# k loaded in long runs and put in order by a VectorE copy, squares made in place, weight words on the attention's load queue, in one core's fused attention and bilinear FFN

## The chip, the cores and the metric

The kernel runs on one core of one Trainium2 chip. The metric is the device time in microseconds (us), the median of the timed runs; the profile is of one more execution of the same program. The core's engines run side by side, each through its own list of instructions in order, and wait for each other by semaphores: TensorE (PE in the profile, with PEld for its weight loads), VectorE (DVE), ScalarE (ACT), GpSimd (POOL) and SyncE (SP), which here only issues DMA transfers. ACT issues DMA transfers too. The transfers of SP appear in the profile as queue q1, those of ACT as q10; both are carried by the same 16 DMA engines.

## The reference: attention with normalized q and k, then a bilinear FFN

```python
batch, n_heads, seq, head_dim = (8, 12, 448, 64)          # attention, fp32
def rmsnorm(x, g):
    rms = np.sqrt(np.mean(x * x, axis=-1, keepdims=True) + 1e-06)
    return x / rms * g
q_n, k_n = (rmsnorm(q, g_q), rmsnorm(k, g_k))
scores = scale * np.matmul(q_n, k_n.transpose(0, 1, 3, 2))
# ... softmax over the keys ...
return np.matmul(attn, v).astype(np.float32)

# bridge: (B,H,S,D) -> (B*S, H*D): 3584 tokens of 768
a = x @ w_a          # 768 x 1536
b = x @ w_b          # 768 x 1536
return (a * b @ w_out).astype(np.float32)                 # 1536 x 768
```

q, k and v are fp32; the FFN's weights arrive as float64 and are read by the kernel as pairs of 32-bit words.

## The kernel before

The kernel is written as a plan: every operation is noted with its engine, an estimated duration, a priority (`key`, smaller is earlier) and the tiles that it reads and writes; a list scheduler then fixes the order of each engine's list before anything runs. A tile has a tag, and a tag has a number of buffers: a new tile can be written only when the last user of the oldest one is done.

```python
# op(engine, us, key, emit, reads, writes, new=tiles opened, kb=..., dmas=...)
TURN = 0.18
LANES = 8
RATE, LANDING = 300.0, 2.0          # the planner's picture of a DMA
```

Attention goes in 24 steps `p` of four heads each. The 448 tokens of a head stand as 64 partitions of 7 tokens (token = 7 * partition + j). The loads of a step:

```python
def loads(p, nm):
    t = tile_of(f"{nm}{p}", nm, 2 if nm == "v" else 1)
    def emit():
        x = ld.tile([P, NT, 2, D] if nm == "k" else [P, 2, NT * D], FP32, tag=nm, ...)
        for w in range(2):
            pair = src[b, h0 + 2 * w:h0 + 2 * w + 2]
            nc.sync.dma_start(x[low_high[w]], pair.rearrange("h (p j) d -> p j h d" if nm == "k" else
                                                             "h (p j) d -> p h (j d)", j=NT))
    op("SP", 0.8 if nm != "k" else 1.4, p - (1.8 if nm == "v" else 2.0), emit, [], [t], new=[t],
       kb=460 if nm != "k" else 800, dmas=2)
```

q and v are read in runs of 7 * 64 * 4 = 1792 B, one for a partition and head. k is put in the order (j, head, d) by the transfer itself, because TensorE transposes two heads of one j together; its runs are 64 * 4 = 256 B. Then normalization:

```python
def normalize(p):                    # key = p - NORM, NORM = 2.5
    def squares(s, nm):
        sq = tile_of(f"sq{nm}{p}", "sq", 1)                  # one buffer for q's and k's squares
        # ACT: sq = Square(x); DVE: rs[p][:, s] = sum over d of sq
        op("ACT", 1.07, key, square, [f"{nm}{p}"], [sq], new=[sq])
        op("DVE", 1.1, key, lambda: nc.vector.tensor_reduce(rs[p][:, s], xs["sq", nm, p], AX, ALU.add), [sq], ...)
    # roots: DVE: mean + 1e-6; POOL: power -0.5     (once for q, once for k)
    # apply: DVE: qn = q * root of q, in the order (j, head, d)   (k's root goes into the exponential's scale)

def transposes(p):
    # PE: pt = transpose of k (7 pieces), then of qn (7 pieces); ACT: copy pt to qkT, q's with the gains as scale
    x = xs["k", p] if n == 1 else qns[p]
    for j in range(NT):
        nc.tensor.transpose(t[:, j * P:(j + 1) * P], x[:, j].rearrange("p h d -> p (h d)"), ident)
```

The scores of a step, their exponentials and the products with v follow in 7 pieces j (`sc`, `ET`, `o`). The sums over the keys (`su`) are products with ones in the first 5 steps; later steps add the pieces up on DVE and POOL first (`ADD_UP`). `invert` spreads the sums over partitions by a small transfer (few<-rec), inverts them on DVE, writes them to DRAM (inv<-few) and brings them back to all partitions (rec<-inv); `divide` multiplies.

The weights are made beside attention. `factors(n)` loads the words of a part in two transfers of 768 KB on ACT's queue, rounds them (ACT once, DVE six times over 128 x 1536), forms sums and differences, and stores the result for the later passes (ACT's queue, 1344 KB):

```python
LOADS = "ACT"
KEEPS = "ACT"
def factors(n, key, early, after):
    for part in range(2):
        def load(part=part):
            queue[LOADS].dma_start(...)                      # words of w_a, w_b or w_out
        op(LOADS, 0.45, key - 0.75, load, after, [f"{row}/{part}"], kb=768)
    # rounding, sums and differences on ACT and DVE, then
    queue[KEEPS].dma_start(kept[n], sts[n]...)

GATES = [0, 2, 4, 4, 5, 5, 7, 7, 8, 8, 10, 10, 16, 18, 21, 21, 27, 32]   # number of the score piece it waits for
seq = [15, 13, 16, 12, 14, 0, 1, 2, 3, 4, 5, 6, 7, 8, 9, 10, 11, 17]     # 0-11: w_a, w_b; 12-17: w_out
def weights(at, after):
    for x, n in enumerate(seq):
        if at == GATES[x]:
            factors(n, x * 0.45 + 1.0, x < 2, [after])
```

The FFN works in four passes of two batches, in a scheme of seven instead of eight products per block; its products (`pq`, then `po`, `a` to `g`) have a lower priority than attention and run on TensorE whenever attention has nothing ready.

Of the kernel before, what the change touches and what calls it, by code (L numbers as in the profile page):

```python
# [9 lines left out]
FP32 = mybir.dt.float32  # L10
U32 = mybir.dt.uint32
I32 = mybir.dt.int32
AF = mybir.ActivationFunctionType
# [12 lines left out]
class Plan:  # L26
# [11 lines left out]
    RATE, LANDING = 300.0, 2.0  # L38
# [132 lines left out]
def kernel(  # L171
# [35 lines left out]
    nc = tc.nc  # L207
# [91 lines left out]
    def fast_body(ld, wk, ps_s, ps_o, ps_mm, dram):  # L299
        plan = Plan()  # L300
        op, tile_of = plan.op, plan.tile
        NORM = 2.5
# [9 lines left out]
        LOADS = "ACT"  # L312
# [3 lines left out]
        ADD_UP = [None, 'DVE', 'POOL', 'DVE', 'POOL', 'DVE', 'DVE']  # L316
# [104 lines left out]
        xs, rs, qns, qkTs, pts, scs, ETs, sums, sus, os_, quads, hTs = ({} for _ in range(12))  # L421
        low_high = [slice(0, D), slice(D, P)]

        def loads(p, nm):
            b, h0 = p // HC, 4 * (p % HC)
            src = {"q": q, "k": k, "v": v}[nm]
            t = tile_of(f"{nm}{p}", nm, 2 if nm == "v" else 1)

            def emit():
                x = ld.tile([P, NT, 2, D] if nm == "k" else [P, 2, NT * D], FP32, tag=nm, name=nm + "_sb", bufs=2 if nm == "v" else 1)  # L430
                for w in range(2):
                    pair = src[b, h0 + 2 * w:h0 + 2 * w + 2]
                    nc.sync.dma_start(x[low_high[w]], pair.rearrange("h (p j) d -> p j h d" if nm == "k" else
                                                                     "h (p j) d -> p h (j d)", j=NT))
                xs[nm, p] = x
            op("SP", 0.8 if nm != "k" else 1.4, p - (1.8 if nm == "v" else 2.0), emit, [], [t], new=[t],
               kb=460 if nm != "k" else 800, dmas=2)

        def normalize(p):
# [8 lines left out]
            def squares(s, nm):  # L448
                sq = tile_of(f"sq{nm}{p}", "sq", 1)

                def square():
                    x = xs[nm, p]
                    t = xs["sq", nm, p] = wk.tile([P, 2 * NT, D], FP32, tag="sq", name="sq")
                    flat = (x.rearrange("p h (j d) -> p (h j) d", d=D) if nm == "q" else
                            x.rearrange("p j h d -> p (j h) d"))
                    nc.scalar.activation(t, flat, AF.Square)  # L456
                op("ACT", 1.07, key, square, [f"{nm}{p}"], [sq], new=[sq])
# [8 lines left out]
            def apply():  # L466
                qns[p] = wk.tile([P, NT, 2, D], FP32, tag="qn", name="qn")
# [4 lines left out]
                    ALU.mult)  # L472
            squares(0, "q")
# [7 lines left out]
            qn = tile_of(f"qn{p}", "qn", 1)  # L481
            op("DVE", 1.15, key, apply, [f"{ms}/q", f"q{p}"], [qn], new=[qn], lock=True)
# [804 lines left out]
```

## Time and profile before

| | before |
|---|---|
| device time, median of 3 runs | 1550.15 us (1547.28 to 1551.54) |
| span of the profiled execution | 1548.6 us |
| attention steps 0 to about 10, with the first weights | 0 to 240 us |
| first FFN pass, almost alone on TensorE | 240 to 400 us |
| attention with FFN products between | 400 to 520 and 740 to 890 us |
| DMA packets | 128866, of which 57860 under 512 B |
| q, k, v: transfers of 224 KB | 48 each |
| words of the weights: transfers of 768 KB | 36 |

How to read it: a span is the time from the first to the last instruction of the profiled execution. An engine's busy time is the union of its instructions. TensorE's matrix products are pipelined and their ends are modelled. DMA share is the mean busy share of the 16 DMA engines in a stretch; it can read a little over 1. The chain of waits follows the last instruction back to whatever released it at each step.

### The profile page before, as it was taken

The page shows a single profiled execution, that of the slowest core. Times are in us where ns is not written, and L with a number is a line of the kernel's source. Part 1 is how long each engine was busy: PE and PEld are TensorE (multiplying, and loading weights), DVE is VectorE, ACT ScalarE, POOL GpSimd, SP SyncE. Part 2 cuts the span into 40 slices and gives each one's busy share as a digit, 9 for nine tenths or more (in the row PEclk, how much of TensorE's full clock was granted, in tenths as well). Part 3 has the DMA queues.
Part 4 walks back from the last instruction along what each step waited for, and adds up shares of the span by engine and source line. Part 5 has one row for each costly group of instructions (what it writes and reads, how often), then busy time and mean ns, then how long its engine had stood idle before and what let it go on. Part 6 is the DMA issues. An engine that isn't in the chain of part 4 may idle for free.

```text
span 1548.6 us, 18051 instructions
## 1 busy us (share of the span) xinstructions
PE 1506.9 (97%) x6996; PEld 822.6 (53%) x6996; DVE 813.7 (53%) x1179; ACT 400.7 (26%) x654; POOL 314.1 (20%) x166
## 2 busy tenths in 40 slices
PE   8988999999999999999999999999999999999998
PEld 5553345555444555555444455555547855555796
DVE  5877869888786412222587543222237622222583
ACT  6767661111567100000445500000041000000000
POOL 3426432111345200011244300000111001000000
PEclk9999999999999999999999999999999999999999
DMA  9897445644445542212345456121226742222343
GB/s 269 240 268 199 97 108 178 218 163 175 143 118 128 150 146 76 103 71 107 102 110 152 114 159 199 72 107 71 95 83 206 247 159 100 79 82 91 111 140 110
DMA packets 128866, 214.74 MB, mean 139 GB/s; under 512 B 57860, under 2 KB 108292, under 8 KB 119044
## 3 DMA queue, kind: packets, MB, share of 16 engines
q1 hardware_dynamic: 100708, 160.02, 35.0%
q10 hardware_dynamic: 28064, 53.48, 9.9%
q8 instruction: 57, 0.93, 0.2%
q14 instruction: 37, 0.30, 0.1%
HBM read 169.08 MB, written 44.21 MB: 138 GB/s over the span
## 4 chain that ended last, share of the span: by engine, by line
PE 82%; DMA 7%; DVE 5%; ACT 3%; issue 1%; POOL 1%; SPq 1%; ACTq 0%; DVEq 0%; POOLq 0%
PE pq L1003 48%; PE po L726 16%; PE sc L515 5%; PE o L537 4%; DMA q_sb<-in_q_dram 2%; PE g L901 2%; PE a L901 2%; ACT ET L521 2%; PE pt L494 2%; DMA rec<-inv 1%; PE b L901 1%; PE su L573 1%; PE e L901 1%; PE d L901 1%; DMA lraw<-in_moe_w_b_dram 1%
## 5 line engine op out<-in xcount | busy, mean ns | idle before, releaser
L1003 PE MATMUL pq<-x,st 128*128 128x448 f32 x2016 | 763.5, 540 | 0.9 <-ACT rec L586 0.9
L1003 PEld LDWEIGHTS pq<-x,st 128*128 128x128 f32 x2016 | 381.2, 190 | 379.5 <-issue 371.2
L521 ACT ACTIVATE ET<-sc,ms 128x448 f32<-128x448 f32 x336 | 191.7, 633 | 92.2 <-PE sc L515 65.6
L515 PE MATMUL sc<-qkT 64*64 64x448 f32 x1344 | 177.2, 544 | 18.0 <-ACT ET L521 10.6
L537 PE MATMUL o<-ET,v_sb 64*64 64x448 f32 x1344 | 187.2, 545 | 7.5 <-ACT ET L521 6.9
L464 POOL TENSOR_TENSOR ms<-ms,expo 128x14 f32<-128x14 f32 x48 | 145.6, 3037 | 188.3 <-DVE ms L462 187.6
L1051 POOL TENSOR_TENSOR hT<-hT,t 128x448 f32<-128x448 f32 x24 | 28.4, 1185 | 744.7 <-DVE t L1049 742.5
L726 PE MATMUL po<-st,hT 128*128 128x384 f32 x504 | 166.4, 487 | 0.0
L726 PEld LDWEIGHTS po<-st,hT 128*128 128x128 f32 x504 | 95.0, 190 | 67.9 <-issue 3.9
L551 POOL TENSOR_TENSOR sum<-sum,ET 128x896 f32<-128x896 f32 x38 | 81.4, 2141 | 139.1 <-ACT ET L521 97.0
L1025 ACT COPY hT<-pq 128x448 f32<-128x448 f32 x24 | 12.8, 532 | 372.9 <-PE pq L1003 372.9
L515 PEld LDWEIGHTS sc<-qkT 64*64 64x64 f32 x1344 | 58.1, 132 | 95.2 <-issue 34.8
L537 PEld LDWEIGHTS o<-ET,v_sb 64*64 64x64 f32 x1344 | 60.2, 132 | 87.9 <-ACT ET L521 42.2
L726 PE MATMUL po<-st,fin 128*128 128x384 f32 x264 | 89.9, 490 | 0.0
L551 DVE TENSOR_TENSOR sum<-sum,ET 128x896 f32<-128x896 f32 x57 | 62.8, 1101 | 26.6 <-POOL sum L551 19.4
L726 PEld LDWEIGHTS po<-st,fin 128*128 128x128 f32 x264 | 49.1, 190 | 39.0 <-issue 7.0
L1063 POOL TENSOR_TENSOR hT<-hT,t 128x448 f32<-128x448 f32 x48 | 58.5, 1219 | 53.7 <-DVE t L1060 45.5
L458 DVE TENSOR_REDUCE ms<-sq 128x14 f32<-128x896 f32 x48 | 51.8, 1079 | 27.7 <-ACT sq L456 27.5
L1056 DVE TENSOR_TENSOR hT<-U,pq 128x448 f32<-128x448 f32 x48 | 29.8, 621 | 66.5 <-PE pq L1003 66.5
L746 DVE TENSOR_TENSOR o_sb<-fin,po 128x384 f32<-128x384 f32 x36 | 20.0, 554 | 80.2 <-PE po L726 72.4
L1060 DVE TENSOR_TENSOR t<-U,pq 128x448 f32<-128x448 f32 x48 | 29.7, 619 | 59.6 <-PE pq L1003 57.3
L1028 ACT COPY t<-pq 128x448 f32<-128x448 f32 x24 | 12.8, 533 | 176.0 <-PE pq L1003 176.0
(117 smaller groups left out, 1297.0 us busy)
## 6 DMA issues: line engine op xcount, KB each, us to landing
st<-kept SPq DMA_DIRECT2D x36, 1344.0 KB
st<-kept_o SPq DMA_DIRECT2D x28, 1152.0 KB
kept<-st ACTq DMA_DIRECT2D x12, 1344.0 KB
ti<-kept_t SPq DMA_DIRECT2D x48, 288.0 KB
q_sb<-in_q_dram SPq DMA_DIRECT2D x48, 224.0 KB
k_sb<-in_k_dram SPq DMA_DIRECT2D x48, 224.0 KB
v_sb<-in_v_dram SPq DMA_DIRECT2D x48, 224.0 KB
rec<-inv SPq DMA_DIRECT2D x48, 224.0 KB
```

Source lines behind the costliest of these rows:

```text
L458: op("DVE", 1.1, key, lambda: nc.vector.tensor_reduce(rs[p][:, s], xs["sq", nm, p], AX, ALU.add), [sq], [f"{ms}/{nm}"])
L464: lambda: nc.gpsimd.tensor_tensor(msf(), msf(), expo[:, 0:2 * NT * (b - a)], ALU.pow), [], names)
L494: nc.tensor.transpose(t[:, j * P:(j + 1) * P], x[:, j].rearrange("p h d -> p (h d)"), ident)
L515: nc.tensor.matmul(t[low_high[w], e, 0:S], lhsT=qkTs[p][low_high[e], 1, j * P + w * D:j * P + (w + 1) * D], rhs=qkTs[p][low_high[e], 0, w ...
L521: nc.scalar.activation(E[:, e], scs[p, j][:, e, 0:S], AF.Exp, scale=rs[p][:, 1, 2 * j + e:2 * j + e + 1])
L537: nc.tensor.matmul(os_[p][low_high[e], w, 0:S], lhsT=xs["v", p][low_high[w], e, j * D:(j + 1) * D], rhs=ETs[p, j][low_high[w], e], start=( ...
L551: two[e].tensor_tensor(sums[p], sums[p] if j > 1 else ETs[p, 0], ETs[p, j], ALU.add)
L726: nc.tensor.matmul(held["po"][:, 0:HALF], lhsT=a[0]()[:, c], rhs=sts[beta, 12 + place_of[f]][:, c], start=(c == 0), stop=(c == MH - 1))
L901: nc.tensor.matmul(held[bank], lhsT=x()[:, c], rhs=y(c), start=(start and c == 0), stop=(stop and c == MI - 1), skip_group_check=True)
L1003: nc.tensor.matmul(banks[bank][:, 0:S], lhsT=sts[at][:, f, c * P:(c + 1) * P], rhs=quads[x][:, c], start=(start and c == 0), stop=(stop an ...
L1056: take("DVE", 0.68, lambda bank=bank, i=i, n=n: V.tensor_tensor(C(i, n), held["U"], PS(bank), ALU.add), [f"p{ident_}.{bank}", U], [hp[i]])
L1063: lambda i=i, n=n, nm=nm: two[TIMES].tensor_tensor(C(i, n), C(i, n), held[nm], ALU.mult), [t], [hp[i]],
```

## The change

k is loaded like q and v, in runs of 1792 B, into a buffer that was the squares'; a copy on VectorE puts it in the order (j, head, d) into the buffer that was k's. k's squares are then made in place, over the raw k, and q's squares in the buffer of qn, which the normalized q overwrites afterwards. So no memory is added. The aim is to spare the DMA engines k's short packets while the weights are streaming in. The words of the weights are now issued by SP, in one list with the attention's loads, instead of by ACT. The order in which the weight parts are made, the score pieces that they wait for, and several priorities are new: loads of q and k 1.5 steps ahead, of v 0.5, normalization 1.5 (2.5 before), the inversion of the sums one step earlier in priority.

```diff
-    RATE, LANDING = 300.0, 2.0
+    RATE, LANDING = 300.0, 2.5
-        NORM = 2.5
+        NORM = 1.5
-        LOADS = "ACT"
+        LOADS = "SP"
+        TURNS = "DVE"
-        ADD_UP = [None, 'DVE', 'POOL', 'DVE', 'POOL', 'DVE', 'DVE']
+        ADD_UP = [None, 'DVE', 'DVE', 'POOL', 'DVE', 'DVE', 'POOL']
 ...
         def loads(p, nm):
-            t = tile_of(f"{nm}{p}", nm, 2 if nm == "v" else 1)
+            home = {"q": "q", "k": "sq", "v": "v"}[nm]
+            t = tile_of(f"{nm}{p}", home, 2 if nm == "v" else 1)
 ...
-                    nc.sync.dma_start(x[low_high[w]], pair.rearrange("h (p j) d -> p j h d" if nm == "k" else
-                                                                     "h (p j) d -> p h (j d)", j=NT))
+                    nc.sync.dma_start(x[low_high[w]], pair.rearrange("h (p j) d -> p h (j d)", j=NT))
-            op("SP", 0.8 if nm != "k" else 1.4, p - (1.8 if nm == "v" else 2.0), emit, [], [t], new=[t],
-               kb=460 if nm != "k" else 800, dmas=2)
+            op("SP", 0.8, p - (0.5 if nm == "v" else 1.5), emit, [], [t], new=[t],
+               kb=460, dmas=2)
+
+        def turn_over(p):
+            kn = tile_of(f"kn{p}", "k", 1)
+            def emit():
+                kns[p] = ld.tile([P, NT, 2, D], FP32, tag="k", name="kn", bufs=1)
+                to, x = kns[p].rearrange("p j h d -> p h j d"), xs["k", p].rearrange("p h (j d) -> p h j d", d=D)
 ...
+                    two[TURNS].tensor_copy(to, x)
+            op(TURNS, {"ACT": 1.07, "DVE": 1.0, "POOL": 1.9}[TURNS], p - NORM, emit, [f"k{p}"], [kn], new=[kn], lock=TURNS != "ACT")
 ...
             def squares(s, nm):
-                sq = tile_of(f"sq{nm}{p}", "sq", 1)
 ...
+                    if nm == "q":
+                        qns[p] = wk.tile([P, NT, 2, D], FP32, tag="qn", name="qn")
+                        t = qns[p].rearrange("p j h d -> p (j h) d")
+                    else:
+                        t = x
+                    nc.scalar.activation(t, x, AF.Square)
 ...
-                    x = xs["k", p] if n == 1 else qns[p]
                     for j in range(NT):
-                        nc.tensor.transpose(t[:, j * P:(j + 1) * P], x[:, j].rearrange("p h d -> p (h d)"), ident)
+                        x = (kns if n else qns)[p][:, j]
+                        nc.tensor.transpose(t[:, j * P:(j + 1) * P], x.rearrange("p h d -> p (h d)"), ident)
 ...
-            op("SP", 0.8, p - 0.0, spread_out, [t], [few], new=[few], kb=20, dmas=2)
+            op("SP", 0.8, p - 1.0, spread_out, [t], [few], new=[few], kb=20, dmas=2)
 ...      (the inversion's other operations likewise: p - 0.0 becomes p - 1.0)
-        GATES = [0, 2, 4, 4, 5, 5, 7, 7, 8, 8, 10, 10, 16, 18, 21, 21, 27, 32]
-        seq = [15, 13, 16, 12, 14, 0, 1, 2, 3, 4, 5, 6, 7, 8, 9, 10, 11, 17]
+        GATES = [1, 2, 3, 4, 4, 6, 6, 7, 10, 10, 10, 13, 14, 16, 17, 17, 20, 24]
+        seq = [12, 16, 14, 13, 15, 0, 1, 2, 3, 4, 5, 6, 7, 8, 9, 10, 11, 17]
 ...
-                    factors(n, x * 0.45 + 1.0, x < 2, [after])
+                    factors(n, x * 0.65 + 0.0, x < 2, [after])
```

## The prediction

> **What bounds the kernel now.** I read the page first: the engines' shares, then the chain that ended last.
>
> ```profile
> PE 1506.9 (97%) x6996; PEld 822.6 (53%) x6996; DVE 813.7 (53%) x1179; ACT 400.7 (26%) x654; POOL 314.1 (20%) x166
> PE 82%; DMA 7%; DVE 5%; ACT 3%; issue 1%; POOL 1%; SPq 1%; ACTq 0%; DVEq 0%; POOLq 0%
> ```
>
> TensorE (PE) is busy for 1506.9 us of a span of 1548.6 us. The change adds and removes no matrix product, so the whole prize is the 1548.6 - 1506.9 = 41.7 us in which PE stands idle, 2.7% of the span. Where that idle time lies comes from the busy time in stretches (columns: stretch, length, then PE, PEld, DVE, ACT, POOL busy, clock, DMA share, GB/s):
>
> ```profile
> 0.00:14.00 14.00, 9.34 (x60) 8.43 (x64) 4.31 (x9) 5.58 (x7) 6.00 (x10) 1.00 0.90 219
> 14.00:60.00 46.00, 44.66 (x429) 26.40 (x425) 37.57 (x42) 35.78 (x55) 17.61 (x5) 1.00 0.92 253
> 60.00:140.00 80.00, 69.83 (x636) 41.08 (x628) 64.29 (x78) 55.21 (x86) 30.23 (x10) 1.00 0.96 273
> 140.00:240.00 100.00, 92.80 (x663) 40.31 (x664) 74.78 (x90) 63.26 (x103) 50.31 (x21) 1.00 0.44 104
> 240.00:400.00 160.00, 160.00 (x498) 79.46 (x497) 140.94 (x157) 31.76 (x39) 24.45 (x17) 1.00 0.48 176
> 400.00:520.00 120.00, 116.82 (x830) 54.54 (x828) 81.85 (x101) 74.83 (x123) 58.11 (x25) 1.00 0.54 138
> 740.00:890.00 150.00, 145.24 (x974) 66.99 (x973) 104.83 (x133) 79.53 (x134) 60.32 (x25) 1.00 0.47 122
> 1130.00:1548.00 418.00, 408.25 (x1645) 262.56 (x1644) 184.78 (x366) 35.73 (x74) 30.62 (x24) 1.00 0.39 129
> ```
>
> Length less PE busy gives the idle time: 4.7 (start), 1.3, 10.2, 7.2, 0, 3.2, 4.8 and 9.8 us (the last has only the end of the last attention step and the end of the kernel). The change concerns attention and the preparation of weights, so it can reach about 10.2 + 7.2 in the first 240 us and 3.2 + 4.8 later: 25 us. In 60 to 140 us neither PE, DVE nor ACT is full, but the DMA engines are, at 0.96. The chain of waits there agrees:
>
> ```profile
> 64.43 10.54 DMA kept_o<-st
> 77.14 8.89 DMA q_sb<-in_q_dram
> 93.51 12.14 DMA lraw<-in_moe_w_b_dram
> 105.72 4.83 DMA few<-rec
> 115.64 5.51 DMA inv<-few
> 121.74 9.73 DMA rec<-inv
> ```
>
> A load of q (0.46 MB) takes 8.9 us there against 3.65 us at 143.57 in the same chain, and the three small transfers of the inverted sums take 20 us in sum. So DMA latency is what sets the idle time of this stretch, through ACT (its squares wait for q) to PE.
>
> [...] Two quiet stretches, the first with one load of k, the second with one of q and one of v:
>
> ```profile
> q1 hardware_dynamic: 1890, 0.46, 39.3%
> q1 hardware_dynamic: 576, 0.92, 56.1%
> ```
>
> The first stretch is 6.0 us, so k takes 0.393 * 6.0 = 2.36 us of all 16 engines; the second is 6.7 us, so q and v take 3.76, 1.88 each. Alone, k costs 0.5 us more than q. [...] k's packets of 256 B take 20 to 30 ns, the weights' packets of 1024 B on the other queue 63 ns (80 to 140 us)[...]; the load issued at 97.0 us has its last packet near 110. [...] the tensor_scalar over 1536 elements takes 953 to 960 ns[...]. [...]
>
> **The change part by part.**
>
> *k in long runs.* 24 loads of 1792 packets become loads of 256. Alone this frees 24 * 0.5 = 12 us of DMA time, 8 loads or about 4 us of it before 140 us. Larger is the latency[...], and not for k only, since q, v and the inverted sums stand behind k in the same ring. PE idles 10.2 us in 60 to 140 for such latencies. I take half: -5 us. After 140 us the DMA share is 0.44, so little: -1 us from this part.
>
> *The copy.* 24 copies [...]: 15 us on DVE, 12 steps or 7.5 us in the first 240 us. DVE is busy 181 of those 240 us, so it fits on average, but in 14 to 60 us DVE is at 37.6/46 = 82%, and the copy stands between the load and the transposition of k. Some copies will wait for GpSimd. +2 us.
>
> *Squares in place.* The same 48 activations (954 ns each); only what they wait for changes. q's squares go into qn's single buffer, so normalization of a step starts only after the transposition of q of the step before; k's squares no longer wait for q's reduction. By the new priorities (1.5 steps ahead instead of 2.5) this is meant. 0 us.
>
> *Words on SP's queue.* 36 issues leave ACT's queue, about 0.4 us each in the timeline, 14 us in all; 20 of them, or 8 us, in the first 240 us. ACT is busy there 160 of 240 us, and PE's waits there are for ACT (exponentials and copies of qkT); some of the issues lie beside ACT's running instruction, so I take -1 us. Against it: words and attention now share one ring in order, so a load of q behind two word loads waits for 1.57 MB, which at the 273 GB/s of the stretch is 5.8 us. This gives back part of the first item: +1 us.
>
> *New order of weights, inversion a step earlier in priority, loads of v later.* The early words start after the first scores (about 14 us) instead of at 9.2 us beside the first loads. The inversion's three transfers go ahead of other loads. -1.5 us in all.
>
> *The later attention stretches* (3.2 + 4.8 us idle; a 6.2 us and a 4.6 us load of q are in the chain at 466 and 482): -1 us.
>
> Sum: -5 - 1 + 2 + 0 - 1 + 1 - 1.5 - 1 = -6.5 us, and I shade it to -6, as the static order that results is the part I can't see. 1550 - 6 = 1544 us.
>
> **The rivals.** *Head of the line:* the words on SP's queue stop the attention's loads, each time the ring has 1.57 MB in it, and SP also waits for the words' place to be free before it can issue the next load of q. For it: SP already waits much for others in order. Against it: the plan orders SP's list with these waits in view. If it wins, some 13 pairs before 240 us cost 1 us each: 1555 to 1560 us. *DVE becomes the bound:* the copies [...] push DVE to its limit in 14 to 140 us, where it is 80% busy; the chain would then go through DVE, and the time be 1552 to 1557. *PE hides it all:* the FFN's products fill the gaps from 140 us on, and before it, PE is 88 to 97% busy; then the time stays at 1548 to 1551. *DMA relief is worth all of it:* most of the 25 us goes: 1528 us.
>
> **Range and chances.** The most that can be won is 41.7 us; faster by 2% (under 1519 us) would need 31 of them, of which only 25 are in reach: 3%. Slower by 2% (over 1581) would need a plan gone wrong: 3%. Otherwise within 2%: 94%. The three runs before differ by 4 us. The range is 1532 to 1556 us: below, two thirds of what is in reach, above, the head of the line at half its cost.
>
> **What would show it.** PE busy should stay near 1507 us. PE's idle time in 60 to 140 us should fall from 10 to about 5, with k's packets of 256 B gone from the packet count (57860 under 512 B to about 15000) and no load of q over 7 us in the chain. The copy should show at about 0.62 us, 24 times[...]. I am wrong if PE's idle time grows in 14 to 140 us with SP's loads in the chain (head of the line), or with DVE's copy in it, or if the gain lies after 890 us, where nothing of the change works.

## The result, and the profile after

The changed kernel took 1555.81 us (median of 4 runs, 1553.9 to 1557.17), the kernel before 1550.0 us beside it (4 runs, 1547.28 to 1551.54): a ratio of 1.004, 95% interval 1.0025 to 1.0055. That is within 2% and inside the predicted range, but it is a loss of 6 us where a gain of 6 us was predicted. The runs below were made on several chips, on which the kernel before took 1546.5 to 1548.0 us; so kernels are compared by their ratio to the kernel before on the same chip.

The page of the changed kernel: busy time of the engines, DMA packets, and the shares of the chain that ended last.

```profile
PE 1508.5 (97%) x6996; PEld 830.4 (53%) x6996; DVE 814.3 (52%) x1203; ACT 400.1 (26%) x654; POOL 306.0 (20%) x166
DMA packets 92002, 214.74 MB, mean 138 GB/s; under 512 B 14852, under 2 KB 71428, under 8 KB 82180
PE 80%; DVE 9%; DMA 3%; ACT 2%; issue 2%; POOL 2%; SPq 1%; ACTq 0%; DVEq 0%; POOLq 0%
```

PE's work is what it was (1506.9 us before). k's short packets are gone: under 512 B there are 14852 instead of 57860. In the chain DMA has fallen from 7% to 3%, and DVE has risen from 5% to 9%. The same stretches as in the prediction (length, then PE, PEld, DVE, ACT, POOL busy, clock, DMA share, GB/s):

```profile
0.00:14.00 14.00, 8.65 (x49) 7.99 (x49) 3.78 (x10) 4.67 (x6) 3.52 (x10) 0.98 0.51 131
14.00:60.00 46.00, 42.98 (x389) 24.31 (x389) 33.17 (x38) 32.19 (x49) 14.85 (x5) 0.89 0.81 259
60.00:140.00 80.00, 69.58 (x647) 41.41 (x645) 67.27 (x82) 55.27 (x86) 24.34 (x8) 1.00 0.91 278
140.00:240.00 100.00, 89.54 (x664) 41.38 (x665) 73.27 (x93) 64.58 (x106) 44.11 (x18) 0.95 0.39 102
240.00:400.00 160.00, 159.82 (x465) 79.95 (x467) 137.12 (x157) 27.34 (x31) 27.17 (x18) 1.00 0.49 176
```

PE's idle time in the first four is 5.35, 3.02, 10.42 and 10.46 us, against 4.66, 1.34, 10.17 and 7.20 before: 29.3 instead of 23.4 us. And the column that the prediction never looked at has changed: TensorE's granted clock is 0.89 in 14 to 60 us and 0.95 in 140 to 240 us, where it was 1.00. After 240 us little more is lost: the 61st product of the first FFN pass, up to which both kernels have done the same products but for 14 transpositions, starts at 239.17 instead of 233.14 us, 6.0 later, and the span ends 1555.3 - 1548.6 = 6.7 later.

Where the lag arises is read from one instruction that each attention step has once, ScalarE's copy of the transposed q (with the gains), by its start in the timelines. The table will serve for the experiments too. Its columns are the start in step 0, then the time from step to step, and from step 10 to the end of the span, all in us; each row is one profiled execution, `after_again` a second one of the changed kernel. The labels of the other rows stand with the experiments below.

| kernel | step 0 | 0 to 5 | 5 to 6 | 6 to 8 | 8 to 10 | 10 to end |
|---|---|---|---|---|---|---|
| before | 12.6 | 106.6 | 17.7 | 37.3 | 39.9 | 1334.5 |
| after | 17.0 | 102.2 | 25.3 | 38.3 | 38.9 | 1333.6 |
| `after_again` | 16.4 | 102.2 | 24.2 | 36.6 | 38.9 | 1333.1 |
| `b_few` | 16.5 | 103.8 | 20.1 | 38.3 | 40.2 | 1338.8 |
| `k_few4` | 16.4 | 102.5 | 20.2 | 35.7 | 38.9 | 1332.5 |
| `n_gains` | 15.2 | 101.1 | 20.6 | 37.1 | 38.9 | 1332.8 |
| `n_k256` | 18.0 | 102.5 | 23.0 | 37.3 | 38.9 | 1335.4 |
| `d_k256` | 16.8 | 102.7 | 24.6 | 38.4 | 38.9 | 1332.6 |
| `c_words` | 16.3 | 106.8 | 19.0 | 37.6 | 38.9 | 1333.4 |
| `i_order` | 16.4 | 110.8 | 14.1 | 39.3 | 35.3 | 1340.4 |
| `j_konly` | 13.6 | 117.7 | 14.2 | 39.8 | 36.7 | 1334.4 |
| `m_recip` | 16.6 | 101.1 | 19.7 | 41.3 | 38.9 | 1339.4 |

So the changed kernel starts 4.4 us late, has made that good by step 5, and then loses 7.6 us between steps 5 and 6 alone. From step 10 on the lists mix attention and FFN products differently, so only the rest as a whole is given.

**The start.** The timelines of SP, DVE and PE of the changed kernel (start, duration, engine, instruction; in brackets the idle time before it and what ended it):

```profile
2.47 0.37 SPq L241 DMA_DIRECT2D grow<-in_g_q_dram  x1
3.18 1.43 SPq L436 DMA_DIRECT2D q_sb<-in_q_dram  x2
...
10.46 0.63 DVE L450 COPY kn<-k_sb 128x896 f32<-128x896 f32 x1 [0.65 <-DMA k_sb<-in_k_dram]
...
15.20 1.73 PE L514 MATMUL pt<-ident,qn 128*128 128x128 f32 x7 [3.07 <-DVE qn L487]
18.09 3.27 PE L535 MATMUL sc<-qkT 64*64 64x448 f32 x16 [1.16 <-ACT qkT L521]
```

and the three lines of the kernel before that answer to the second and the last two:

```profile
0.74 1.44 SPq L433 DMA_DIRECT2D q_sb<-in_q_dram  x2
...
11.51 0.98 PE L494 MATMUL pt<-ident,qn 128*128 128x128 f32 x7 [1.24 <-DVE qn L468]
13.65 1.73 PE L515 MATMUL sc<-qkT 64*64 64x448 f32 x16 [1.16 <-ACT qkT L501]
```

With the new priorities (q and k 1.5 steps ahead instead of 2) the two loads of the gains come ahead of q in SP's list. They write a small tile that ScalarE clears first, at 2.03 to 2.44 us, so q's first load is issued at 3.18 instead of 0.74. The copy of k then stands in DVE's list until k lands, ahead of the root of q. The first scores start 18.09 - 13.65 = 4.4 us later (how much of it is due to the gains' loads is measured below); and the same seven transpositions that took 0.98 us before take 1.73 here.

**Steps 5 to 6.** SP's, DVE's and PE's timeline of the changed kernel:

```profile
126.37 1.13 SPq L383 DMA_DIRECT2D lraw<-in_moe_w_b_dram  x2
127.60 1.71 SPq L613 DMA_DIRECT2D few<-rec  x2
...
140.42 0.25 DVE L626 RECIPROCAL few<-few 112x16 f32<-112x16 f32 x1 [6.98 <-DMA few<-rec]
...
141.53 1.08 DVE L487 TENSOR_TENSOR qn<-q_sb,ms 128x896 f32<-128x896 f32 x1
...
142.76 1.73 PE L514 MATMUL pt<-ident,qn 128*128 128x128 f32 x7 [6.14 <-DVE qn L487]
```

Step 4's spreading transfer (few<-rec, a few KB) is issued directly behind a pair of words (1.57 MB) on the same queue and lands 11 us after its issue has ended (127.60 + 1.71 to 140.4). The reciprocal heads DVE's list and waits 6.98 us for it; behind it in the list stands the normalized q of step 6, and PE waits 6.14 us for that.

The words alone don't make up the 11 us. By the trace's packets 1.26 of the 1.57 MB of words have moved by 134 us. Then ScalarE's queue (q10) comes in with a store of a weight part (kept<-st, 1.38 MB, issued at 129.10). From 134 to 137 us (queue, packets, MB, share of 16 engines):

```profile
q10 hardware_dynamic: 111, 1.19, 93.5%
q1 hardware_dynamic: 113, 0.12, 10.8%
```

The two queues moved about as many packets, 111 and 113; but a packet of the store has 10.75 KB and one of the words 1 KB, so the store moved 1.19 MB and the words 0.12. The tail of the words hardly moved until the store was done (its last packet ended at 137.7 us), and the first packet of the small transfer went at 137.3 us.

What follows is seen in stretches of 4 us (length, PE busy, clock, DMA share, GB/s):

```profile
132.00:136.00 4.00, 3.83 (x37) 1.00 1.09 411
136.00:140.00 4.00, 0.62 (x7) 0.97 0.93 268
140.00:144.00 4.00, 1.24 (x6) 0.50 0.03 5
144.00:148.00 4.00, 3.96 (x27) 0.67 0.47 134
```

After the stop the granted clock is 0.5 until 146.6 us. Apart from the end of the span, the changed kernel's trace has three stretches at 0.5 (13.5 to 23.7, 139.8 to 146.6, 160.3 to 163.7 us), at stops of PE of 3.07, 6.14 and 3.38 us. They are 10.24, 6.83 and 3.41 us long, that is 3, 2 and 1 times 3.413, and they lie on one grid of that length: 139.8 - 13.5 = 37 * 3.413 and 160.3 - 139.8 = 6 * 3.413. The kernel before, whose longest wait of PE before 240 us is 2.5 us, has none there. In the three PE is busy for 7.4 + 3.8 + 3.4 = 14.6 us; at half the clock that costs an estimated 7.3 us at most. Idle time (5.9 us more) and clock together would be 13 us; the loss is 6. PE's busy time up to 233.14 us before and 239.17 us after is 209.8 and 209.9 us, so what the half clock cost came back as shorter busy time elsewhere; where is not shown. The stretches are no accident of this one execution: the mean granted clock is 0.992 to 0.994 in all nine executions of the changed kernel, and 0.998 to 0.999 in the 11 of the kernel before beside the last five of them.

### The profile page after: what moved, and what is told of

Same layout as the page of the kernel before. It is cut to its first block, busy times and chain, and to the rows that moved or that the text cites. A ratio compares the mean times of both kernels' runs of the same rounds, so it can differ in the third digit from the quotient of the medians.

```text
span 1555.3 us, 18108 instructions
## 1 busy us (share of the span) xinstructions
PE 1508.5 (97%) x6996; PEld 830.4 (53%) x6996; DVE 814.3 (52%) x1203; ACT 400.1 (26%) x654; POOL 306.0 (20%) x166
## 2 busy tenths in 40 slices
DMA packets 92002, 214.74 MB, mean 138 GB/s; under 512 B 14852, under 2 KB 71428, under 8 KB 82180
## 4 chain that ended last, share of the span: by engine, by line
PE 80%; DVE 9%; DMA 3%; ACT 2%; issue 2%; POOL 2%; SPq 1%; ACTq 0%; DVEq 0%; POOLq 0%
PE pq L1023 48%; PE po L746 14%; PE o L557 5%; PE sc L535 4%; PE g L921 2%; PE a L921 2%; PE pt L514 1%; PE su L593 1%; ACT ET L541 1%; DMA rec<-inv 1%; PE b L921 1%; DVE fin L734 1%; POOL sum L571 1%; PE e L921 1%; PE d L921 1%
## 5 line engine op out<-in xcount | busy, mean ns | idle before, releaser
L484 POOL TENSOR_TENSOR ms<-ms,expo 128x14 f32<-128x14 f32 x48 | 136.0, 2844 | 171.9 <-DVE ms L482 155.8
L535 PEld LDWEIGHTS sc<-qkT 64*64 64x64 f32 x1344 | 62.3, 135 | 82.3 <-issue 35.1
L557 PEld LDWEIGHTS o<-ET,v_sb 64*64 64x64 f32 x1344 | 61.5, 134 | 78.1 <-issue 38.9
L746 PEld LDWEIGHTS po<-st,fin 128*128 128x128 f32 x264 | 49.3, 190 | 38.9 <-issue 7.0
L271 ACT ACTIVATE st<-lraw 128x1536 f32<-128x1536 f32 x16 | 26.3, 1645 | 109.9 <-PE pq L1023 109.9
```

Source lines behind the costliest of these rows:

```text
L484: lambda: nc.gpsimd.tensor_tensor(msf(), msf(), expo[:, 0:2 * NT * (b - a)], ALU.pow), [], names)
L535: nc.tensor.matmul(t[low_high[w], e, 0:S], lhsT=qkTs[p][low_high[e], 1, j * P + w * D:j * P + (w + 1) * D], rhs=qkTs[p][low_high[e], 0, w ...
L557: nc.tensor.matmul(os_[p][low_high[e], w, 0:S], lhsT=xs["v", p][low_high[w], e, j * D:(j + 1) * D], rhs=ETs[p, j][low_high[w], e], start=( ...
L746: nc.tensor.matmul(held["po"][:, 0:HALF], lhsT=a[0]()[:, c], rhs=sts[beta, 12 + place_of[f]][:, c], start=(c == 0), stop=(c == MH - 1))
```

## The experiments

All edits are to the changed kernel unless said. The first theory was: the words on SP's queue delay the small transfer and the start is late; the copy and the long runs matter little. Rivals: the start and the clock (`a_gains`, `e_warm`), the queue of the words (`c_words`), the copy on DVE (`l_turn_act`), the planner's new order (`h_inv0`, `i_order`), the k part itself (`d_k256`, `j_konly`).

**The gains' loads on ScalarE's queue (`a_gains`).**

```diff
-            nc.sync.dma_start(grow[:, n], g.rearrange("(o d) -> o d", o=1))
+            nc.scalar.dma_start(grow[:, n], g.rearrange("(o d) -> o d", o=1))
```

> The changed kernel, with only the two small loads of the gains issued by ACT instead of by SP, every other list in the same order. Theory of the start (the gains' loads, now ahead of q in SP's list, wait for ACT and hold q back by 2.4 us; PE then idles and its granted clock falls to a half from 13.5 to 23.7 us): first scores at about 15.5 instead of 18.1 us, a shorter or no stretch at half clock before 30 us, and if nothing later absorbs it 3 to 6 us less: 1550 to 1553 us. Rival (the whole loss lies in the gap at 136 to 160 us; the lag of the start, which is gone by step 5, is absorbed): the first scores come earlier all the same, but the time stays at 1555 to 1557 us.

Measured: 1.004 (1.0026 to 1.0053), as without. The first scores start at 16.40 instead of 18.09 us, so the gains' loads held up 1.7 of the 4.4 us (1.1 of 3.8 against `after_again`, where the scores start at 17.49); no run separates the rest. In this one the square of q stands in ScalarE's list behind the copy of the gain (7.49 us), and the square of k waits for DVE's copy of k. The stretch at half clock at the start is gone and step 5 starts at 116.0 us, where two traces of the changed kernel have 119.2 and 118.7. Against the second of these the lead is gone by step 8 (179.5 us in both), but the two differ by 3 us there themselves (182.8 and 179.5), so one trace can't say where a gain of this size went. The stop between steps 5 and 6 is there as before (24.9 us). By the times the edit can't be told from nothing.

**The spreading transfer on ScalarE's queue, in all 24 steps (`b_few`).**

```diff
-                    nc.sync.dma_start(fews[0][e * FEW:(e + 1) * FEW],
+                    nc.scalar.dma_start(fews[0][e * FEW:(e + 1) * FEW],
```

> The changed kernel, with the transfer that spreads the key sums (3.5 KB, twice a step) issued by ACT instead of by SP, so that it doesn't stand behind words, q, k and v in SP's ring; PE's, DVE's and GpSimd's lists are the same. Theory of the ring (the reciprocal in DVE's list waits 7 us for this transfer at 133 to 140 us, the normalized q behind it, PE idles 6.1 us and falls to half clock): the wait of the reciprocal falls under 1 us, no half clock from 139 to 164 us, 6 to 10 us less: 1546 to 1550 us. Rival (DVE is too full, the copies of k are what holds it): the gap at 136 us stays, with the copy or the reduction before it, and the time stays at 1554 to 1558 us.

Measured: 1.0092 (1.0076 to 1.0107), slower. Steps 5 to 6 took 20.1 us, as wished, but ScalarE's timeline shows what the pair of issues costs where exponentials are waited for:

```profile
38.51 2.22 ACTq L613 DMA_DIRECT2D few<-rec  x2
40.83 1.16 ACT L541 ACTIVATE ET<-sc,ms 128x448 f32<-128x448 f32 x2 [1.92 <-issue]
```

PE then stands still for 2.54 us and has half its clock from 41.2 to 44.6 us. By step 10 this is made good (218.9 us, against 221.7 and 218.4 in the two traces of the changed kernel); the run falls behind after it, with 1338.8 us to the end instead of 1333.6 and 1333.1. Whether it is the pairs of the later steps that cost this is not shown. ScalarE's queue for all steps is no way out.

**The words on ScalarE's queue again, all else new (`c_words`).**

```diff
-                        queue[LOADS].dma_start(to, moe_w_out[k * P:(k + 1) * P, :])
+                        nc.scalar.dma_start(to, moe_w_out[k * P:(k + 1) * P, :])
```

(and the same for w_a and w_b.)

> The changed kernel, with the words' transfers issued by ACT at the same places, as before the change; all other lists the same. Theory of the ring: the same small transfers no longer stand behind 1.57 MB of words, the gap at 136 us goes, but ACT pays about 0.4 us an issue and may wait for the words' place: 1548 to 1553 us. Rival (it isn't the ring but the new order of DVE's list): the gap at 136 us stays and the time stays at 1554 to 1558 us or grows.

Measured: 1.0046 (1.0033 to 1.006). The stop between steps 5 and 6 is gone (19.0 us), and another has come: at 25.80 us ScalarE's issue waits for the place of the words, and the exponentials behind it wait 4.49 us.

```profile
25.80 2.89 ACTq L380 DMA_DIRECT2D lraw<-in_moe_w_out_dram  x2
28.74 1.16 ACT L541 ACTIVATE ET<-sc,ms 128x448 f32<-128x448 f32 x2 [4.49 <-DMA hraw<-in_moe_w_out_dram]
```

So steps 0 to 5 take 106.8 instead of 102.2 us, 4.3 of the 4.6 us of it between steps 0 and 1: it is this one issue that waits, not the time of all the issues, that the change took from ScalarE, and what SP's queue gives there it takes back at step 6.

**k in 256 B runs, straight into its order; the copy stays (`d_k256`).**

```diff
-                    nc.sync.dma_start(x[low_high[w]], pair.rearrange("h (p j) d -> p h (j d)", j=NT))
+                    nc.sync.dma_start(x[low_high[w]], pair.rearrange("h (p j) d -> p j h d" if nm == "k" else "h (p j) d -> p h (j d)", j=NT))
```

(with the views of the copy, the squares and the scale to match.)

> The changed kernel, with k loaded again in runs of 256 B, straight into the order (j, head, d); the copy on DVE stays, so only the length of the runs differs. If long runs are worth the 5 us that the prediction gave them in 60 to 140 us: the lag against the kernel before, which is 4.4 us at the first scores and 0 at step 5, stays at 4 us or more, and the time is 1558 to 1563 us. Rival (the recovery by step 5 comes from the new order, not from the runs): 1554 to 1558 us.

Measured: 1.0062 (1.0049 to 1.0076), against 1.004 and 1.0049 of the changed kernel: intervals that overlap. In the table it differs from the changed kernel's first trace by about a microsecond at most in every column. Not settled here, and taken up below.

**The changed kernel once more (`after_again`), and idle products ahead of the first transpositions (`e_warm`).**

> The changed kernel once more, beside the kernel before and the next three on one chip: 1.0025 to 1.0055 of the kernel before, and the same three stretches at half clock (13.5 to 23.7, 139.8 to 146.6, 160.3 to 163.7 us, each within 1 us). If these stretches come from chance and not from the program's order, they lie elsewhere.

Measured: 1.0049 (1.0036 to 1.0062). Two of the three stretches at half clock are there (13.2 to 23.5 and 139.5 to 146.4 us), the third is not; PE's stop at 155 us is 2.94 us long, where the first trace has one of 3.38 at 156. This and the stop between steps 5 and 6 (5.00 instead of 6.14 us) are most of what the two traces differ by at step 8.

```diff
+                    if p == 0:
+                        for x in range(7 if n else 10):
+                            nc.tensor.matmul(warms[0][:, 0, 0:P], lhsT=ident, rhs=ident, start=True, stop=True)
```

> The changed kernel, with 17 more idle products of the identity on PE before the first two transpositions (7 and 10), so that PE isn't idle from 9 to 15 us. They are extra work that no result needs. Theory of the clock (half speed from 13.5 to 23.7 us costs half of the 7.4 us that PE is busy in it): no half clock before 30 us, first scores at 18 us as in the changed kernel, but step 1 about 3.5 us earlier, and 2 to 4 us less in the end. Rival (the start's lag is absorbed by step 5, so its clock doesn't matter): the time of the changed kernel within 1 us.

Measured: 1.0043 (1.003 to 1.0056), not told apart from the line above. The stretch at the start shrank from 10.2 to 3.4 us; step 5 came 1.2 us earlier (117.5 against 118.7), step 6 only 0.3 (142.54 against 142.85): here the stop between them took most of it.

**The inversion's old priority (`h_inv0`).**

```diff
-            op("SP", 0.8, p - 1.0, spread_out, [t], [few], new=[few], kb=20, dmas=2)
+            op("SP", 0.8, p - 0.0, spread_out, [t], [few], new=[few], kb=20, dmas=2)
```

(and the three lines after it.)

> The changed kernel, with the inversion's priority of before (the step's own, not one step earlier). The planner makes a new order of all lists. Theory of the ring and of DVE's order (a reciprocal placed early in DVE's list waits for a small transfer behind the words, and holds the normalized q): without the early place no 7 us wait of the reciprocal and no gap over 3 us at 130 to 145 us, 5 to 9 us less: 0.998 to 1.001 of the kernel before. Rival (the words in SP's ring hold whatever comes next, inversion or not): another gap of 3 us or more between 60 and 170 us with a transfer behind words in the chain, 1.003 to 1.006.

Measured: 1.0055 (1.0042 to 1.0068). The planner put the reciprocal at the same place in DVE's list near 140 us, where it waits 6.26 us for the same transfer, so the run says only that going back on this priority does not mend it.

**The k part alone, on the kernel before (`j_konly`):** long runs, copy and squares in place; old queue, order and priorities.

> The kernel before, with the part on k alone: long runs, the copy on DVE, squares in place; words on ACT, old order of weights, old priorities. If long runs are worth 5 us and the losses come from the other parts: 0.995 to 0.998 of the kernel before, no half clock. Rival (the squares in place and the copy tie normalization to the step before, and this is the loss): 1.002 to 1.006.

Measured: 1.0092 (1.0067 to 1.0116), as slow as the slowest of all runs. Its profile shows the copy waiting at the head of DVE's list for k, and PE's waits before 240 us are for exponentials (engine, line, what for, us in total, times, longest):

```profile
22.85 0.63 DVE L450 COPY kn<-k_sb 128x896 f32<-128x896 f32 x1 [0.74 <-DMA k_sb<-in_k_dram]
...
38.41 0.63 DVE L450 COPY kn<-k_sb 128x896 f32<-128x896 f32 x1 [1.26 <-DMA k_sb<-in_k_dram]
```

```profile
PE o L557 <- ACT ET L541: 15.1, 10, 4.6
```

It loses 11 us in steps 0 to 5 (117.7 against 106.6). The copy's own waits are too short to be that; whether the squares in place or the order that the planner made of it costs more is not shown. Planned with the old parameters, the k part is a loss, and the other parts of the change are what makes it bearable.

**Only step 4's spreading transfer on ScalarE's queue (`k_few4`).**

```diff
-                    nc.sync.dma_start(fews[0][e * FEW:(e + 1) * FEW],
+                    (nc.scalar if p == 4 else nc.sync).dma_start(fews[0][e * FEW:(e + 1) * FEW],
```

> The changed kernel, with the spreading transfer of step 4 alone issued by ACT (the one behind which the reciprocal waits 7 us at 133 to 140 us); all other lists the same. ACT's cost in the other 23 steps, which made the run with all of them on ACT slower, is away. Theory of the ring: the gap at 136 us shrinks from 6 to under 2 us, no half clock from 139 to 147 us, 4 to 8 us less than the changed kernel: 0.999 to 1.002 of the kernel before. Rival (the loss is a backlog of DVE, which only shows at this gap): the gap goes, but the time it frees comes back as idle time before 240 us, 1.003 to 1.006.

Measured: 1.0017 (1.0008 to 1.0026). ScalarE's issue and DVE's timeline, to be read beside that of the changed kernel:

```profile
128.97 2.26 ACTq L613 DMA_DIRECT2D few<-rec  x2
...
135.37 0.25 DVE L626 RECIPROCAL few<-few 112x16 f32<-112x16 f32 x1 [0.74 <-DMA few<-rec]
...
136.48 1.08 DVE L487 TENSOR_TENSOR qn<-q_sb,ms 128x896 f32<-128x896 f32 x1
```

The wait of 6.98 us is 0.74, steps 5 to 6 take 20.2 us, and in this execution no half-clock stretch is left but the one at the start. It is the fastest of 15: its time is 1548.03 us at a mean clock of 0.996, the slowest took 1553.36 at 0.992. One transfer of a few KB on another queue is worth 0.2 to 0.3%, by the two measurements of the changed kernel, so half to two thirds of the loss; the interval stands clear of that of `after_again` and just touches that of the first. What the other queue saves here is the place in the line behind 1.57 MB: the transfer lands 4.1 us after its issue has ended (131.2 to 135.3) instead of 11. It also goes ahead of the store, which ScalarE now issues at 131.32 us, behind it.

**The old order of the weights, with the new queue and priorities (`i_order`).**

```diff
-        GATES = [1, 2, 3, 4, 4, 6, 6, 7, 10, 10, 10, 13, 14, 16, 17, 17, 20, 24]
+        GATES = [0, 2, 4, 4, 5, 5, 7, 7, 8, 8, 10, 10, 16, 18, 21, 21, 27, 32]
```

(and the sequence and its slope.)

> The changed kernel, with the weights' order, gates and priorities of before. The planner makes a new order of all lists. Theory of DVE's backlog (the words come 7 us later, so DVE's first rounding starts at 30 instead of 18.5 us, and DVE is then 93% busy from 60 to 120 us and sets the steps): rounding starts at 20 us or earlier, DVE under 88% from 60 to 120 us, 0.997 to 1.001 of the kernel before. Rival (the order of the weights is fitted to the new queue and is no cause): 1.004 to 1.012.

Measured: 1.0065 (1.0046 to 1.0084), no gain, and not told apart from the changed kernel's 1.004 and 1.0049. Rounding starts at 18.18 us as hoped, but DVE is still 93% busy from 60 to 120 us. Steps 0 to 5 take 110.8 instead of 102.2 us, and more than that comes back at steps 5 to 6 (14.1 instead of 25.3): at step 10 this run is at 215.9 us, 5.7 ahead of the changed kernel. It falls behind later, with 1340.4 us to the end instead of 1333.6, and PE idle for 7.4 us in 400 to 520 us instead of 3.2. As all lists are new, the run doesn't say what the order of the weights is worth by itself.

**The copy of k on ScalarE (`l_turn_act`).**

```diff
-                if TURNS == "ACT":
+                if True:
```

> The changed kernel, with the 24 copies of k made by ACT at the same places of the emitted order instead of by DVE; PE's, SP's and GpSimd's lists the same. If the 15 us of copies on DVE are what holds the attention steps (DVE 93% busy from 60 to 120 us): 3 us or more less, 1.000 to 1.003 of the kernel before. If they lie in DVE's slack: 1.004 to 1.009, as ACT now has about 1 us more in each step.

Measured: 1.0047 (1.003 to 1.0065), the same as on DVE. A copy takes a median of 939 ns on ScalarE. So it is not the load of the copies on DVE that loses the time, unless they cost as much on ScalarE. On DVE eight of the 24 are long; one of them, with the line of GpSimd beside it in the changed kernel:

```profile
165.36 2.30 DVE L450 COPY kn<-k_sb 128x896 f32<-128x896 f32 x1 [0.42 <-PE pt L514]
165.08 2.09 POOL L571 TENSOR_TENSOR sum<-sum,ET 128x896 f32<-128x896 f32 x1 [2.46 <-DVE sum L571]
```

**The reciprocal two places later in DVE's list (`m_recip`)** (a pass over the finished lists, which moves each reciprocal, and what depends on it, behind the next two DVE instructions):

```diff
+            while seen < 2 and j + 1 < len(order):
+                j += 1
+                seen += ops[order[j][1]][0] == "DVE"
 ...
+            order[i:j + 1] = rest + moved
```

> The changed kernel, with each of the 24 reciprocals moved two instructions back in DVE's list (and the two transfers that depend on it as far as they must); PE's, ACT's and GpSimd's lists keep their order. Theory (it is the place of the reciprocal in DVE's list, ahead of the normalized q, that turns a slow small transfer into a stop of PE): the wait at 133 to 140 us no longer holds the normalized q, gap under 2 us there, 4 to 8 us less than the changed kernel: 0.999 to 1.002 of the kernel before. Rival (what follows needs the inverted sums just as soon, or the transfer's ring holds q and k too): the gap moves to another instruction, 1.003 to 1.006.

Measured: 1.0066 (1.0048 to 1.0085). The stop moved into SP's list: the transfer after the reciprocal is ahead of q's load there. From the chain of waits (start, duration, what):

```profile
128.00 10.96 DMA few<-rec
...
139.05 0.27 DVE few L641
...
139.33 0.34 SPq L633
...
140.97 3.59 DMA q_sb<-in_q_dram
```

The load of q is issued only at 139.78 us. Steps 5 to 6 were short (19.7), steps 6 to 8 long (41.3), together as long as in `after_again` (60.8). What this run loses beyond that comes after step 10 (1339.4 us to the end), from a cause that is not shown. So the transfer itself must come earlier; to wait for it elsewhere does not help.

**With the stop away: the start and the long runs again.** Each is `k_few4` with one of the edits above: idle products (`n_warm`), gains' loads (`n_gains`), 256 B runs (`n_k256`), and the first two together (`n_gains_warm`).

> The changed kernel with step 4's spreading transfer on ACT, and with the 17 idle products on PE before the first transpositions (extra work that no result needs). If the start's clock is the rest of the loss and nothing swallows it now: half clock before 25 us for at most 4 us, 2 to 3 us less than with step 4's transfer alone: 0.999 to 1.001 of the kernel before. If later steps swallow it still: 1.001 to 1.0025.

> The changed kernel with step 4's spreading transfer and the two loads of the gains on ACT. If the start's order is the rest of the loss: first scores near 16.4 us at full clock, 2 to 4 us less than with step 4's transfer alone: 0.998 to 1.001 of the kernel before. If later steps swallow it: 1.001 to 1.0025.

> The changed kernel with step 4's spreading transfer on ACT, and k loaded in runs of 256 B as before the change (the copy on DVE stays). If long runs are worth what the prediction gave them (5 us in 60 to 140 us, with nothing to swallow it): 1.004 to 1.006 of the kernel before. If they are worth little: 1.001 to 1.003.

> The changed kernel with step 4's spreading transfer and the gains on ACT, and with the 17 idle products on PE. If gains first and clock are both part of the loss, this is the fastest: 0.997 to 1.000 of the kernel before. If the gains alone suffice, the same as without the idle products within 1 us; if the idle products hold the first transpositions up, 1 to 2 us more.

Measured on one chip, to be compared with `k_few4` on another (1.0017, 1.0008 to 1.0026) by the ratios to the kernel before: idle products 1.0004 (0.9995 to 1.0013), gains' loads 0.9999 (0.9991 to 1.0007), 256 B runs 1.0038 (1.0024 to 1.0053), both of the first two 1.0015 (1.0008 to 1.0022). The gains' loads, not to be told from nothing in the changed kernel, are worth 0.18% now, with intervals that do not touch; by the second measurement below (1.0003, 0.9994 to 1.0011) it is 0.14%, with intervals that just overlap. The idle products point the same way with intervals that overlap. Together they undo each other: with q early, the idle products hold the first transpositions up (step 0 at 18.7 us).

Long runs of k are worth 0.0038 - 0.0017 = 0.2%, some 3 us, with intervals that just overlap; the 0.13 to 0.22% between `d_k256` and the changed kernel agree. In the two traces the difference is not in steps 0 to 5, where the DMA engines are busiest (share 0.91 from 60 to 140 us in the changed kernel; 102.5 us both), but in steps 5 to 6 (23.0 against 20.2). There PE's wait for an exponential is 3.54 instead of 2.97 us, and a stretch at half clock follows it (134.1 to 140.9 us) that `k_few4` does not have. By the estimate above the profiled execution with 256 B runs loses up to 9.4 us to the clock, that of `k_few4` up to 3.1. But these two traces are the slowest of 6 executions (1556.86 us, median 1554.70) and the fastest of 15 (1548.03, median 1550.71), so they show more than the 3 us, and part of what they show is chance; the place of the gain is not settled.

**The last stop.** In all these variants PE waits some 3 us near 150 us for exponentials. In DVE's list four subtractions of the FFN's quarters (2.6 us) and the next qn stand ahead of the sum that frees an exponential's buffer. The last two runs, on one chip, are `n_gains` again (`n_gains_2`) and `n_gains` with these four moved behind qn, two sums and a reciprocal (`o_comb`); all other lists are the same.

```diff
+        is_combine = lambda n: ops[n][0] == "DVE" and ops[n][1] == 0.63 and ops[n][3].__qualname__.split(".")[-3] == "combine"
 ...
+                group = [x for x in range(i, len(order)) if is_combine(order[x][1])][:4]
 ...
+                order[i:j + 1] = rest + moved
```

> The changed kernel with step 4's spreading transfer and the two gains' loads on ScalarE's queue, and besides it the first group of four subtractions of the quarters (2.6 us of DVE near 146 us) moved behind qn, two sums and a reciprocal in DVE's list; all other lists are the same. Theory (the last stop of PE near 150 us, 3.2 us at o<-ET, is these four standing before the sum that frees an exponential's buffer): that stop falls under 1 us, no half-clock stretch from 151 to 154, 3 to 4 us gained: ratio 0.998 to before, 1545 us. Rival (a later wait swallows it, as the first FFN's products or the next k or q do): the stop goes but the time stays, 1.000. Rival (the four are needed at once by the FFN): slower, 1.001.

> The same without the move of the four subtractions, for the comparison on one chip: 0.9999 of before as on the other chip, within 0.001.

Measured: 1.0007 (0.9999 to 1.0014) with the move, 1.0003 (0.9994 to 1.0011) without. PE's timeline without the move:

```profile
151.50 1.20 PE L557 MATMUL o<-ET,v_sb 64*64 64x448 f32 x5 [3.45 <-ACT ET L541]
```

and with it, PE and DVE (its lines are numbered 20 higher):

```profile
148.35 1.12 PE L577 MATMUL o<-ET,v_sb 64*64 64x448 f32 x5 [1.02 <-ACT ET L561]
...
159.67 1.77 PE L613 MATMUL su<-sum,ones 64*64 64x448 f32 x8 [3.77 <-POOL sum L591]
...
150.43 4.38 DVE L702 TENSOR_TENSOR x<-x 128x448 f32<-128x448 f32 x4
```

The stop of 3.45 us fell to 1.02, so the reading was right; and a stop of 3.77 us came one step later, with the half-clock stretch behind it (159.7 to 163.1 us instead of 152.4 to 155.8), because the four (4.38 us there instead of 2.60) now hold the later sums and the copy of k. The time stays, as the first rival had it. No version found beats the kernel before.

## Why the prediction was right or wrong

- **PE's work, the packets, the copy: right.** PE is busy for 1508.5 us (about 1507 said), packets under 512 B are 14852 (about 15000 said), and the copy takes a median of 624 ns, 24 times (0.62 us said, an estimate of the author's that no copy in the trace of before showed). That some copies would wait for GpSimd was right too: eight of the 24 take 1.08 to 2.52 us, and each of the eight starts while a sum is running on GpSimd and ends after it (as at 165.36 us, shown with `l_turn_act`). So the copies take 26.5 us of DVE, not 15. Their cost of +2 us in the kernel's time is not shown: with the 24 copies on ScalarE instead, the time is the same.
- **k in long runs, -5 us in 60 to 140 and -1 later: wrong in place, half right in size.** With 256 B runs steps 0 to 5 are as long (102.5), so the latency beside the weights, on which the -5 rests, sets nothing there in this order; how much of it short packets cost was the author's estimate, not shown by the trace of before. (The load issued at 97.0 us, with its last packet near 110, had its first only at 103.0: it took 7.2 us, and the rest was waiting in line. And rec<-inv, counted among the small transfers, moves as much as a load of q, twice 224 KB.) In all, the long runs are worth some 3 us, in the traces after 120 us. In the changed kernel itself they point the same way within overlapping intervals.
- **Words on SP's queue, -1 and +1: both far too small.** By `c_words`, ScalarE's freedom is worth 4.6 us in steps 0 to 5, nearly all of it one issue that would have waited. The head of the line cost some 4 to 5 us (steps 5 to 6: 25.3 and 24.2 against 20.2 in `k_few4`), by the 0.2 to 0.3% of that run. The rival of that name had the mechanism right, but spread it over 13 pairs (the 20 issues counted in the sum are 10) at 1 us each and over loads of q; what `k_few4` mends is one pair, once, and the one that stood behind it was the small spreading transfer. That a store on the other queue would hold the words up (0.12 MB of them from 134 to 137 us) was not foreseen.
- **New order and inversion, -1.5: wrong.** That the inversion's transfers "go ahead of other loads" was read from priorities; in the list that came out, step 4's stands right behind 1.57 MB. The start was taken to gain and lost 4.4 us, 1.1 to 1.7 of them because the gains' loads, which wait for ScalarE, came ahead of q. These loads cost 0.14 to 0.18% by the two runs of `n_gains`. From step 0 to step 5 the changed kernel gains 4.4 us; what the weights' order has to do with it is not shown (`i_order`).
- **Not in the sum: the clock.** The prediction had its column in the stretches, at 1.00 throughout, and did not ask whether it would stay there; in the changed kernel it was 0.89 in 14 to 60 and 0.95 in 140 to 240 us. By the estimate above up to 7.3 us went there.
- **PE's idle time in 60 to 140 falling from 10 to 5: wrong** (10.4). The condition for being wrong was that PE's idle time grows in 14 to 140 us with SP's loads in the chain. It grew, 11.5 to 13.4 us, and SP's transfers were in the chain: rec<-inv (7.15 us at 73.75), few<-rec (5.62 at 84.50) and, at the stop, a load of k (7.27 at 133.25). No load of q is over 7 us (4.51 at 124.37), as said. The chain names k at the stop, until 140.52 us, but the reciprocal had started at 140.42; and in `k_few4` qn starts at 136.48 us, before the first packet of that load of k (137.3), so k is not what it waits for.
- **The later attention, -1: no gain.** In 400 to 520 and 740 to 890 us PE is idle for 3.2 and 4.0 us, against 3.2 and 4.8, and the end is 6.7 us late where the first FFN pass was 6.0.

So the steps that failed are the words' queue and the new order: what a static order does with one queue was put down as small terms that cancel (-1, +1, -1.5), and it is the result. The loss of 0.4 to 0.5% is made up of 0.2 to 0.3 (the small transfer, shown by `k_few4`) and 0.14 to 0.18 (the gains' loads at the start, by `n_gains` against `k_few4`, on different chips). With both mended the kernel is where the one before is, 0.9999 and 1.0003, although the long runs are in it. What eats their 0.2% may be the stop near 150 us; with that stop down to 1.02 us another took its place, so this stays open.

## What to carry to other kernels

A small transfer on which the next stage hangs should not share a queue with transfers of a megabyte: look for what stands ahead of it in the ring, and move that one transfer, not all of its kind. When a planned order is changed, read the lists that come out, each engine's head and what stands behind it, not the priorities that went in. And try a small edit again once the large stop after it is gone: the gains' loads could be told from nothing only then.

## What the runs showed of the hardware

- A few KB behind 1.57 MB in one queue landed 11 us after the issue had ended; issued on the other queue in the same stretch it landed 4.1 us after (131.2 to 135.3 in `k_few4`), while the DMA engines were as full (share 1.09 and 1.12 from 132 to 136 us). Part of the 11 us was a store of 1.38 MB on the other queue: from 134 to 137 us it moved 111 packets of 10.75 KB, 1.19 MB, against 113 of 1 KB, 0.12 MB.
- The length of a stop alone did not tell whether the clock would fall: waits of 2.54 (`b_few`) and 2.94 us (`n_warm`) were followed by a stretch at half clock, one of 3.13 us (`k_few4`, 150.23 to 153.36 us, clock 1.00 from 144 to 158 us) was not, and in `n_warm` the clock fell at 118.5 us, where PE had waited 1.10 us just before. What decides it is not shown. In the changed kernel's trace the three stretches begin and end on one grid of 3.413 us. A stretch of 3.4 us at a clock of 0.5 costs an estimated 1.7 us at most beyond the stop itself, half its length. It may be part of why two traces of the changed kernel differ by 3 us at step 8; this was not tested.
- A copy on DVE that starts while a sum runs on GpSimd takes 1.08 to 2.52 us instead of 0.62, and ends 0.48 to 0.49 us after that sum (eight of 24 in the changed kernel, seven in each of `after_again` and `k_few4`). A copy in which such a sum starts keeps its 0.62 us (six of 24).
- The issue of a pair of small transfers took 2.2 us of ScalarE's list in `b_few` and 1.7 us of SP's in the changed kernel: not small beside an exponential of 0.64 us.
